# Attention backward loop: one hand-written order of PE's work for another

## The chip, the cores and the metric

The kernel runs on one core of a Trainium2 chip. The time is the device time of one launch, in microseconds (us); the kernel before took 2461.13 us, the median of three runs (2459.82 to 2464.63).

A core has five engines, each with its own queue of instructions that it takes in order. PE (TensorE) multiplies matrices and writes PSUM; ACT (ScalarE) computes functions such as the exponential; DVE (VectorE) works elementwise; POOL (GpSimd) does elementwise work on SBUF; SP (SyncE) issues DMAs. ACT issues DMAs too, from the same queue as its computing. The engines run side by side and wait for each other by semaphores. [...]

## The reference

The kernel computes a transformer block with adaptive layer norm and the gradients of all its inputs but one:

```
mod = (silu(c) @ w_mod).reshape(c.shape[0], 6, 1, -1)       # sa, ca, ga, sb, cb, gb
h = layernorm(x) * (1 + ca) + sa
x = x + ga * attention(h, wqkv, wo)                          # 32 heads of 16, no mask
h = layernorm(x) * (1 + cb) + sb
x = x + gb * (relu(h @ w1 + b1) ** 2 @ w2 + b2)
out, vjp = jax.vjp(f, A_x, A_wqkv, A_wo, B_w1, B_b1, B_w2, B_b2, c, w_mod)
return (out, *vjp(grad_out))
```

There are 2048 tokens of 512 features, and the MLP has 1792. Inputs and outputs are bf16. The part that matters here is the gradient of the attention. For each head, with scores S = q k^T / 4 and their softmax P, and with dP = dO v^T less a sum per row, it needs P again, dS = P * dP, and from them dV = P^T dO, dK = dS^T q and dQ = dS k.

## The kernel before

The first 1100 us are the forward pass and the MLP's gradients. Then the backward loop of the attention runs to about 2350 us, and the last 110 us finish the input and weight gradients. The change touches the backward loop alone.

**Tiling.** The 32 heads go in 8 groups (hg) of 4. A *unit* is one group, 128 queries (one of 4 qi in one of 4 qc) and 512 keys (kc). Four units with the same keys and neighbouring queries are a *block*; there are 512 units and 128 blocks. The four heads of a unit sit in four groups of 32 rows of the 128 partitions, so a head's matmul takes 32 rows.

**The steps of a unit, and the token that stands for each.**

- s0 to s15 (`score`): one matmul each, the scores of one head of one unit; s0 to s3 are the heads of the block's first unit, s4 to s7 of the second, and so on. A score goes to one of three PSUM banks, A, B or C, by a letter per token behind the order.
- e0 to e15 (`expo`): ACT reads such a bank, takes the exponential and writes E_u in SBUF as bf16. The row sums of the forward pass are already in the operands, so E is P.
- D (`dp_pair`): PE computes dP of two heads into a PSUM tile psD (there are two), and DVE multiplies it with E into dS_u. The Ds run behind: the first D of a block is the second pair of the last unit of the block before, the other seven belong to the block itself up to the first pair of its last unit. After the second pair of some units, SP issues a DMA that transposes dS into dsT (`transpose_unit`).
- q: alternately `k_quad` (k, four matmuls, dS times q) and `v_quad` (v, four matmuls, E times dO), each on four groups of 32 columns, both summed in the bank accVK. The qs run further behind, the first of a period being k of the third unit of the block before. After every 16 units ACT copies accVK to vkb.
- t1, t2 (`pe_turn`): in every second block one unit's dS is transposed on PE instead, in two halves of eight 128 x 128 transposes each, into bank C; T1 and T2 are ACT's copies of these into dsT.
- d1, d2 (`dq_quad`): two halves of eight matmuls, dS^T times k for the block two before, into bank C; Q (`dq_out`) is ACT's copy to dqtmp, which POOL adds to dQacc. At the end of a head group, POOL's result dQst is stored to DRAM by four DMAs that ACT issues.
- f (`keep_warm`): one matmul with zeros, which changes no result.

**The order.** All this is under a manual schedule: the loop at L1783 goes through the tokens of a block in the written order and each call puts its instructions on its engine's queue. Blocks alternate between `order_t`, which has t1, t2, T1, T2 and f, and `order_n`, which has none of them; the two are one period, and there are 64 periods. As each engine takes its own queue in order, a token binds only the tokens of the same engine ahead of it and behind it; everything else is data, or a bank or buffer that must be free. Bank C serves a score, a turn or dQ in turn, and in the stretches where it holds a turn or dQ the scores have A and B alone.

**Loads and stores on ACT's queue.** The operands of the next head group, the stores of vkb and those of dQst are put on ACT's queue through a list of due times (`at`, `todo`), which is counted in Ds: after the n-th D, what is due at n is issued. `dq_out` books the four stores of a finished head group at 6, 7, 8 and 9 Ds after its own place.

The lines of the loop that dispatch the tokens:

```
for b in range(NU // 4 + 3):
    toks, bank = order_t if on_pe(b - 1) else order_n
    for tok in toks:
        c, i = tok[0], int(tok[1:] or 0)
```

Of the kernel before, what the change touches and what calls it, by code (L numbers as in the profile page):

```python
# [21 lines left out]
D = 512  # L22
# [12 lines left out]
def kernel(  # L35
# [1546 lines left out]
    with ExitStack() as ph:  # L1582
# [9 lines left out]
        def load_head(hg):  # L1592
            st = dict(hsets[hg % 2])
            st["qz"] = qz[hg % 2]
            st["acc"] = stg.tile([P, n], F32, name="dQacc", tag="dQacc", bufs=1)
            st["dq"] = stg.tile([P, n], BF, name="dQst", tag="dQst", bufs=1)
            st["vk"] = stg.tile([P, n], BF, name="vkb", tag="vkb")
            hst[hg] = st
# [140 lines left out]
        def dq_out(b):  # L1739
# [21 lines left out]
                    at(cur["j"] + 6 + hq, load, dQc[hg // 2, r:r + DH, :], st["dq"][32 * hq:32 * hq + DH, :])  # L1761

        order_t = (
            "s0 s1 q s2 e0 e1 D s3 D e2 s4 e3 q t1 e4 T1 D "
            "s5 s6 e5 f f t2 e6 s7 T2 e7 D s8 e8 D f f s9 e9 q q s10 "
            "s11 e10 D d1 d2 e11 Q q s12 D e12 s13 e13 q s14 D e14 "
            "s15 q q e15 ").split(), "ABCABBABACABABCA"
        order_n = (
            "s0 D s1 q e0 q s2 e1 e2 D s3 s4 q s5 e3 D e4 "
            "e5 s6 q s7 D s8 e6 e7 d1 e8 s9 D d2 e9 q Q s10 "  # L1770
            "s11 e10 D q s12 e11 e12 s13 e13 D q s14 s15 e14 e15 D q ").split(), "CBACBACBABABCABC"
        load_head(0)
        for hg in range(1, HG):
            plan_head(hg)
# [332 lines left out]
```

## Time and profile before

One execution was profiled. It took 2461.76 us, with a span of 2460.0 us from its first to its last instruction.

| what | value |
|---|---|
| median of three runs | 2461.13 us |
| profiled execution; its span | 2461.76 us; 2460.0 us |
| busy over the span: PE, ACT, DVE, POOL | 94%, 93%, 75%, 20% |
| mean granted clock of PE | 0.990 |
| exponentials (E_u): number, mean of one in banks A, B, C | 2048; 651, 642, 647 ns |
| dS multiplies: number, mean of one | 1024; 1218 ns |
| copies of a turn (dsT): number, mean of one | 126; 1055 ns |
| copies of dQ (dqtmp): mean of one | 629 ns |
| copies of accVK (vkb): number, mean of one | 32; 688 ns |

An instruction's duration reaches from its start to its end, and on ACT the next one starts before the last has ended: exponentials of 0.65 us end 0.49 us apart. Durations must therefore not be added up; the distance between ends tells what one costs. PE's matmuls overlap in the same way, and their ends are modelled, so its busy share tells little of how much room it has. The name ahead of the arrow is what an instruction writes, the one behind what it reads; a releaser in square brackets is what ended the idle time ahead of it.

### The profile page before, as it was taken

The numbers are of one execution on the slowest core, as the hardware profiler recorded it, in microseconds if no ns is written. First come the engines' busy times: TensorE is split into PE (matmuls) and PEld (weight loads), VectorE is DVE, ScalarE is ACT, GpSimd is POOL, SyncE is SP. The second block draws the span as 40 slices with busy tenths as digits, with TensorE's granted clock in tenths as the row PEclk, the third lists the DMA queues.
The fourth block names the chain that finished last, engine by engine and source line by source line (L and its number), as shares of the span: only waits on it lengthen the run. The fifth ranks groups of instructions, "written<-read, shape, count | busy, mean of one in ns | idle before, by whom it ended". The sixth has DMA issues, their size and how long they took to land.

```text
span 2460.0 us, 49911 instructions
## 1 busy us (share of the span) xinstructions
PE 2308.8 (94%) x18994; PEld 776.1 (32%) x18994; DVE 1846.2 (75%) x2393; ACT 2298.6 (93%) x3559; POOL 489.5 (20%) x661
## 2 busy tenths in 40 slices
PE   8899999989998999899999999999999999999999
PEld 3232223233322333442322323332232332323254
DVE  6555463455445554669999999999899999999975
ACT  7999999999999999639999999999999999999964
POOL 2111222432544353200111101111011010110100
PEclk9999999999999999999999999999999999999999
DMA  4468554266647774989999999999999999999995
GB/s 149 130 171 189 182 140 103 85 161 142 97 91 154 152 139 89 239 244 189 206 198 207 199 212 199 208 196 207 198 201 208 207 206 201 209 195 219 200 261 180
DMA packets 1192303, 440.58 MB, mean 179 GB/s; under 512 B 1068283, under 2 KB 1161913, under 8 KB 1191550
## 3 DMA queue, kind: packets, MB, share of 16 engines
q1 hardware_dynamic: 1155214, 392.23, 81.0%
q0 software_dynamic: 19872, 27.09, 6.9%
q10 hardware_dynamic: 16976, 18.07, 3.0%
q8 instruction: 149, 2.44, 0.4%
q14 instruction: 92, 0.75, 0.1%
HBM read 98.83 MB, written 72.63 MB: 70 GB/s over the span
## 4 chain that ended last, share of the span: by engine, by line
ACT 39%; PE 36%; issue 10%; DVE 8%; DMA 6%; POOL 1%; ACTq 0%; SPq 0%; DVEq 0%; POOLq 0%
ACT E_u L1634 24%; ACT ET L580 12%; PE dqacc L1736 4%; PE psST L578 3%; PE psS_A L1628 3%; DMA dsT<-dS_u 3%; PE accVK L1709 2%; PE pm L234 2%; PE psS_B L1628 2%; PE oacc L594 2%; PE psS_C L1628 2%; PE pm L502 2%; PE pdh L1929 2%; PE pm L412 2%; PE pwq L1962 2%
## 5 line engine op out<-in xcount | busy, mean ns | idle before, releaser
L1650 DVE TENSOR_TENSOR dS_u<-psD_u,E_u 128x1024 bf16<-128x1024 f32 x1024 | 1185.6, 1218 | 63.4 <-PE psD_u L1648 17.4
L580 ACT ACTIVATE ET<-psST 128x1024 bf16<-128x1024 f32 x1024 | 942.4, 1248 | 12.4 <-PE psST L578 12.1
L1634 ACT ACTIVATE E_u<-psS_A 128x512 bf16<-128x512 f32 x768 | 499.8, 651 | 8.2 <-PE psS_C L1628 6.8
L1634 ACT ACTIVATE E_u<-psS_B 128x512 bf16<-128x512 f32 x768 | 493.1, 642 | 11.6 <-DMA dsT<-dS_u 4.6
L1648 PE MATMUL psD_u<-iv,ido 32*128 32x512 bf16 x2048 | 409.2, 386 | 0.3 <-DVE dS_u L1650 0.2
L578 PE MATMUL psST<-qt_sb,kt_sb 32*128 32x512 bf16 x2048 | 311.2, 386 | 39.4 <-ACT ET L580 35.0
L1634 ACT ACTIVATE E_u<-psS_C 128x512 bf16<-128x512 f32 x512 | 331.5, 647 | 3.4 <-PE psS_B L1628 1.1
L1628 PE MATMUL psS_B<-ik,iq 32*128 32x512 bf16 x768 | 293.0, 381 | 13.8 <-ACT E_u L1634 6.2
L1628 PE MATMUL psS_A<-ik,iq 32*128 32x512 bf16 x768 | 292.0, 380 | 13.2 <-DVE dwlast L238 0.9
L1757 POOL TENSOR_TENSOR dQacc<-dQacc,dqtmp 128x512 f32<-128x512 f32 x64 | 81.2, 1269 | 846.3 <-ACT dqtmp L1752 846.3
L1628 PEld LDWEIGHTS <-iq 32*128 32x128 bf16 x2048 | 130.8, 91 | 323.8 <-issue 308.2
L1709 PE MATMUL accVK<-dS_u,qz 128*32 128x512 bf16 x2048 | 213.4, 389 | 0.2 <-DVE dS_u L1650 0.2
L594 PE MATMUL oacc<-ET,vaug 128*32 128x512 bf16 x2048 | 207.1, 395 | 3.9 <-DVE ostage L598 3.9
L1718 PE MATMUL accVK<-E_u,dOs_tok 128*16 128x512 bf16 x2048 | 202.3, 384 | 0.0
L1628 PE MATMUL psS_C<-ik,iq 32*128 32x512 bf16 x512 | 194.2, 379 | 3.9
L578 PEld LDWEIGHTS <-kt_sb 32*128 32x128 bf16 x2048 | 84.2, 91 | 318.2 <-issue 298.6
L1736 PE MATMUL dqacc<-dsT,KS_tok 128*32 128x512 bf16 x2048 | 145.8, 382 | 15.5 <-ACT E_u L1634 1.5
L252 DVE COPY part<-pm 128x512 f32<-128x512 f32 (+2 forms) x106 | 65.2, 615 | 119.2 <-PE pm L234 114.1
L1648 PEld LDWEIGHTS <-ido 32*128 32x128 bf16 x2048 | 106.0, 91 | 96.9 <-issue 84.8
L1821 ACT ACTIVATE dsT<-ptT 128x1024 bf16<-128x1024 bf16 x126 | 132.9, 1055 | 0.1
L1709 PEld LDWEIGHTS <-qz 128*32 128x32 bf16 x2048 | 58.6, 94 | 176.3 <-issue 161.3
L594 PEld LDWEIGHTS <-vaug 128*32 128x32 bf16 x2048 | 53.2, 93 | 121.9 <-issue 121.9
(421 smaller groups left out, 2659.9 us busy)
## 6 DMA issues: line engine op xcount, KB each, us to landing
p_st<-part POOLq DMA_DIRECT2D x36, 256.0 KB, 4.6
kt_sb<-qkT_st POOLq DMA_DIRECT2D x124, 64.0 KB, 3.2
wA<-in_B_w_dram SPq DMA_DIRECT2D x28, 256.0 KB
wB<-w1T_st SPq DMA_DIRECT2D x21, 256.0 KB
wA<-w2T_st SPq DMA_DIRECT2D x21, 256.0 KB
wB<-in_B_w_dram SPq DMA_DIRECT2D x21, 256.0 KB
p_st<-part POOLq DMA_DIRECT2D x28, 192.0 KB, 5.1
p_st<-part SPq DMA_DIRECT2D x18, 256.0 KB
```

Source lines behind the costliest of these rows:

```text
L578: PE.matmul(ps[:, hi, :], kt_sb[r:r + 32, kt * P:(kt + 1) * P], qt_sb[r:r + 32, :], start=True, stop=True, tile_position=(r, 0))
L580: ACT.activation(ET[:, 2 * pair:2 * pair + 2, :], ps[:], AF.Exp, scale=SCALE)
L594: PE.matmul(oacc[32 * hq:32 * hq + 32, :], lhsT, ET[:, hq, :], start=(kt == 0), stop=(kt == TT - 1), tile_position=(0, 32 * hq), skip_grou ...
L1628: PE.matmul(psS[:], st["q"][r:r + 32, qt * P:(qt + 1) * P], st["k"][r:r + 32, kc * 512:kc * 512 + 512], start=True, stop=True, tile_positi ...
L1634: ACT.activation(bst[u][0][:, hq, :], sst.pop((u, hq))[:], AF.Exp, scale=SCALE)
L1648: PE.matmul(psD[:, hi, :], st["do"][r:r + 32, qt * P:(qt + 1) * P], st["v"][r:r + 32, kc * 512:kc * 512 + 512], start=True, stop=True, til ...
L1650: DVE.tensor_tensor(dS_u[:, 2 * pair:2 * pair + 2, :], psD[:], E_u[:, 2 * pair:2 * pair + 2, :], ALU.mult)
L1709: PE.matmul(cur["vk"][32 * hq:32 * hq + 32, :], hst[hg]["qz"][:, qt, hq, :], bst[u][1][:, hq, :], start=(qt == 0), stop=False, tile_positi ...
L1718: PE.matmul(acc[32 * hq:32 * hq + DH, :], dOs_tok[:, qt, (hg * 4 + hq) * DH:(hg * 4 + hq + 1) * DH], E_u[:, hq, :], start=False, stop=(qt ...
L1736: PE.matmul(acc[32 * hq:32 * hq + 32, :], KS_tok[:, kc * 4 + kt, h * DH:h * DH + 32], tT[:, :, hq * 4 + kt, :], start=(kt == 0), stop=(kt ...
L1757: POOL.tensor_tensor(dst2, dst, tmp[:], ALU.add)
L1821: ACT.activation(dst, pt[:], AF.Identity)
```

## The change

Both strings of tokens are written anew. The letters that give the banks, the functions and everything else are the same. The numbers of tokens are the same too but for f, of which `order_t` has five instead of four, and q, of which it has seven instead of eight while `order_n` has nine instead of eight; over a period there are sixteen qs as before.

```
         order_t = (
-            "s0 s1 q s2 e0 e1 D s3 D e2 s4 e3 q t1 e4 T1 D "
-            "s5 s6 e5 f f t2 e6 s7 T2 e7 D s8 e8 D f f s9 e9 q q s10 "
-            "s11 e10 D d1 d2 e11 Q q s12 D e12 s13 e13 q s14 D e14 "
-            "s15 q q e15 ").split(), "ABCABBABACABABCA"
+            "s0 s1 f e0 s2 e1 q s3 e2 s4 e3 D D t1 f q f e4 s5 D T1 s6 "
+            "e5 t2 q e6 T2 f D s7 s8 e7 e8 f D s9 e9 q D s10 s11 d1 "
+            "e10 d2 s12 e11 D Q s13 e12 q e13 s14 D e14 q s15 q e15 ").split(), "ABCABBABACABABCA"
         order_n = (
-            "s0 D s1 q e0 q s2 e1 e2 D s3 s4 q s5 e3 D e4 "
-            "e5 s6 q s7 D s8 e6 e7 d1 e8 s9 D d2 e9 q Q s10 "
-            "s11 e10 D q s12 e11 e12 s13 e13 D q s14 s15 e14 e15 D q ").split(), "CBACBACBABABCABC"
+            "s0 s1 D q e0 e1 q s2 s3 e2 D q e3 s4 s5 D e4 s6 e5 e6 q q "
+            "s7 D e7 s8 d1 s9 e8 e9 D d2 s10 D Q s11 e10 e11 q s12 e12 "
+            "q D s13 e13 s14 q e14 D s15 q e15 ").split(), "CBACBACBABABCABC"
```

In PE's sequence, the first D of a period now stands behind s4 instead of s2; t1 is followed by f, v, f and only then s5; where two qs stood together, mostly one stands now; v of the block's last unit before comes ahead of the sixth D; and k behind d2 has gone to behind s13 in `order_t` and behind s11 in `order_n`.

## The prediction

> **What bounds the kernel now.** The page's first part first, then busy time by stretches of the backward loop (1130 to 2350 us).
>
> ```profile
> PE 2308.8 (94%) x18994; PEld 776.1 (32%) x18994; DVE 1846.2 (75%) x2393; ACT 2298.6 (93%) x3559; POOL 489.5 (20%) x661
> ...
> 1200.00:1300.00 100.00, 96.44 (x926) 29.98 (x922) 95.54 (x84) 98.59 (x190) 11.43 (x9) 1.00 1.18 204
> 1900.00:2000.00 100.00, 96.49 (x940) 30.21 (x933) 95.66 (x84) 98.79 (x190) 11.62 (x8) 1.00 1.18 209
> ```
>
> In the loop three engines look full: PE 96, DVE 96, ACT 99 of 100 us, at clock 1.00. So the shares do not say which is the limit, and I went to the timeline. I call a block run by order_t T, one run by order_n N; two blocks are a period and there are 64. The turns' copies give the period: the first one starts at 1515.65 and again at 1534.83, 19.18 us. Over 59 periods the median is 19.18 without the copy vkb and 19.34 with it, the mean 19.44.
>
> ACT's ends: exponentials follow each other by 0.49 (the copies of dqacc and accVK too), a turn's copy by 0.917. So a period without vkb needs 32 x 0.49 + 2 x 0.917 + 2 x 0.49 = 18.49 on ACT. 0.69 is lost, nearly always in the same five places. Two of them in T, then two in N:
>
> ```profile
> 1519.38 0.69 ACT L1634 ACTIVATE E_u<-psS_C 128x512 bf16<-128x512 f32 x1
> ...
> 1520.04 0.60 ACT L1634 ACTIVATE E_u<-psS_A 128x512 bf16<-128x512 f32 x1
> 1520.12 1.05 PE L1736 MATMUL dqacc<-dsT,KS_tok 128*32 128x512 bf16 x16
> 1520.53 0.59 ACT L1634 ACTIVATE E_u<-psS_B 128x512 bf16<-128x512 f32 x1
> ...
> 1521.28 0.60 ACT L1752 ACTIVATE dqtmp<-dqacc 128x512 f32<-128x512 f32 x1 [0.15 <-PE dqacc L1736]
> ...
> 1508.21 0.61 PE L1736 MATMUL dqacc<-dsT,KS_tok 128*32 128x512 bf16 x8
> 1508.45 0.69 ACT L1634 ACTIVATE E_u<-psS_A 128x512 bf16<-128x512 f32 x1
> 1508.76 0.38 PE L1628 MATMUL psS_B<-ik,iq 32*128 32x512 bf16 x1
> 1509.18 0.60 ACT L1634 ACTIVATE E_u<-psS_B 128x512 bf16<-128x512 f32 x1
> 1509.80 0.60 ACT L1752 ACTIVATE dqtmp<-dqacc 128x512 f32<-128x512 f32 x1
> ```
>
> T: e9 leaves bank C at 1520.07, d1 starts in it 0.05 later, both halves run, and Q ends at 1521.88, 1.81 after e9, where e10, e11 and Q alone need 1.47. N: d1 holds PE when s9 is due; s9 starts at 1508.76, e9 ends 1.02 later, 0.15 late; Q then waits 0.11. Medians: e10 of T 0.08, Q of T 0.23 (only without vkb), e0 of N 0.08 (its bank C is left by e14, two before), e9 of N 0.15, Q of N 0.11: together 0.65. These are waits for a bank, not for PE's load.
>
> PE's load: priced by groups that did not wait, the T order takes 8.6 and the N order 6.6, 15.2 of 19.18. PE counts as busy because its matmuls overlap.
>
> SP is the fourth full engine:
>
> ```profile
> L1669 SPq DMA_TRANSPOSE dsT<-dS_u x191: 4821/5332/7152, 1111.3 to 2344.3; - x191
> L1667 SPq DMA_TRANSPOSE dsT<-dS_u x63: 1836/2846/4053, 1127.8 to 2336.8; - x63
> ```
>
> 3 x 5.33 + 2.85 + 4 gaps of 0.1 = 19.2 per period, so SP runs 0 to 10 us behind DVE. And once per head the four stores of dQst disturb ACT:
>
> ```profile
> 1282.85 1.10 ACTq L1610 DMA_DIRECT2D dQc<-dQst  x1
> ...
> 1284.00 0.60 ACT L1634 ACTIVATE E_u<-psS_B 128x512 bf16<-128x512 f32 x1 [0.53 <-issue]
> ...
> 1752.56 3.85 SPq L1667 DMA_TRANSPOSE dsT<-dS_u  x1
> ...
> 1756.56 0.31 ACTq L1610 DMA_DIRECT2D dQc<-dQst  x1
> ...
> 1756.92 0.60 ACT L1634 ACTIVATE E_u<-psS_B 128x512 bf16<-128x512 f32 x1 [4.05 <-DMA dsT<-dS_u]
> ```
>
> The fourth store waited for a transpose to land; that period took 24.70. Summed over all periods, what lies above 19.18 and 19.34 is 10.8 us. That is all that a better order could win.
>
> **The change part by part.** Each engine sees only its own tokens. ACT's e0 to e15, T1 (after e4), T2 (after e6) and Q (after e11 in T, e9 in N) stand in the same sequence before and after, so the exponentials are not reordered on ACT. DVE's 16 multiplies, SP's transposes and POOL's adds keep their sequence. What changes is PE's sequence, one more keep-warm matmul f in T (5 for 4), and between which ACT instructions the ACT-issued DMAs fall.
>
> Prices on PE, start to start: row-tiled group (s, D) to column-tiled one (q, f, d) 0.30; q to q 0.22; column to row 0.33; t to a row group 0.55; matmuls of different row groups start together, a second one on the same group 0.2 later. A bank or psD buffer is taken 0.05 after it is left; an exponential ends 1.02 after its score starts, if it waits; a dS multiply starts 0.54 after its D (1521.32, 1521.86) and the next follows by 1.13.
>
> *The five waits.* T: "s9 ... s10 s11 d1 d2" still puts both halves ahead of Q, and d1 is free to start when e9 leaves C: the D that now stands before s10 ends that group 0.13 before. N: "s8 d1 s9 D d2" is the same. s0 of N still waits for e14. So all five stay: 0.
>
> *q singly, f added.* Row segments per period go from 16 to 19 and PE's load to about 16.6 (three more streams of 0.21, six more changes of mode at 0.10, f 0.22). Covered by PE's 4 us of waiting, unless a score comes late. So I went through every score of the new order, from the release of its bank to its exponential's turn on ACT. Room is left by at least 0.1 everywhere but here:
> - e5 of T. s4 starts 0.05 after e1; the second D behind it shares its row group, 0.2; t1 0.31 later; t1 to f is in no row, between d's 0.44 and 0.55; f to v 0.22, v to f 0.22, f to s5 0.33, then 1.02: 2.79 to 2.90. ACT arrives after e2, e3, e4, T1, e5: 1.47 + 0.917 + 0.49 = 2.88. Late by 0 to 0.02. Before, no f stood there and s5 came straight behind t1 and D.
> - e7 of N. s6 0.05 after e3, k 0.30, v 0.22, s7 0.33, 1.02: 1.92 of 1.96. In time by 0.04.
> - d1 of N, behind an s8 that shares D's row group: 0.09 before e6 leaves C.
> - s10 of T, behind a D that needs a psD buffer. T's first D now stands behind s4 and its multiply starts 0.6 later than before (DVE idles there 0.9 instead of 0.35); the multiplies follow from there by 1.13, so the D ahead of s10 (the sixth) waits to about 0.05 after s10's bank is free. e10 comes 0.05 late, and Q, late by 0.23 anyway, takes that up; with vkb between e9 and e10 it is hidden.
>
> I take 0.02 per period for the first, as t to f changes between 128-wide and 16-wide tiles and is nearest to the 0.55: 64 x 0.02 = 1.3 us. With every step at its largest (0.1 more on each of the first three) they give 0.12 + 0.06 + 0.01 = 0.19, 12 us; the lower end is 0, since the five waits bar a gain here.
>
> *DVE and SP.* DVE needs 16 x 1.13 = 18.1 of 19.18, so the later start is made up within T, where DVE idled before (medians 0.18, 0.16 and 0.46, ahead of the third, fourth and sixth multiply behind t1). T's pair of units 0 and 1 reaches SP 0.5 later, and where SP had caught up it starts 0.5 later. The landing is next wanted by d1 two blocks on, some 8 us after it. Cost 0.
>
> *Stores and loads on ACT's queue.* In N, Q now stands behind one more D, and the stores are counted in Ds: each falls one D later. The first stood behind T1 with a load just ahead of it, and e5 was late by 0.63 in four heads and 0.40 in one: 2.9 us. It now stands alone behind T2, whose 0.917 covers it: -2.9. The fourth now meets a load, between e11 and Q of T: the two take 0.34 + 1.10 there at worst, against 0.49 + 0.23 of room, +0.7 x 6 = +4.2, at best 0. I take 0 for both together, ends -2.9 and +4.2. The fourth store's long wait (5.5 us once) depends on how far SP is behind: 0, ends -5.5 and +5.5.
>
> Sum: 2461.76 (profiled execution: span 2460.0 and 1.76 around it) + 1.3 = 2463.1. The median of the three runs, 2461.13, is 0.6 below it: **2462.5 us**.
>
> **Rivals.**
> 1. *Slower: s5 comes late.* One mechanism: t1, f, v, f stand between s4 and s5, where t1 and D stood. If t to f or the shared row group costs 0.1 to 0.2 more than priced, e5 is late in all 64 periods; it decides from 0.08 on (5 us). At 0.15: 9.6 us, 2471. For it: that path has no slack by my own prices, and t to f was never seen. Against: the largest rows give 2.90 of 2.88.
> 2. *Slower: PE becomes the bound.* 40 mode changes for 34, each 0.10, three more streams, one f: 1.4 per period, 90 us, 2551. For it: PE at 96%. Against: PE's groups fill 16.6 of 19.18. [...]
> 3. *Slower by SP.* Where SP starts 0.5 later in every period and does not catch up, more stores wait as at 1756: two more are 11 us, 2472.
> 4. *Faster.* The disturbances at the heads go: first stores 2.9 and the long wait 5.5, 2453. For it: both hang on where the stores fall. Against: only 10.8 us are there, and half came once.
>
> **How the numbers follow.** Forecast (within 0.2%, 5 us, about what a measurement of this kernel tells from no change; own range 2457 to 2466): 0.42. Rival 1: 0.28; rival 2: 0.04; rival 3: 0.06; rival 4: 0.20. So faster 0.20, same 0.42, slower 0.38. The low end is rival 4, 2453; the high end the largest steps and stores, 12 + 4 above: 2477. Outside: rival 2 and parts of 1 and 4.
>
> **What would show it.** Periods of 19.18 and 19.34 again and the five waits unchanged; e5 of T at most 0.05 late; DVE idle by 0.9 behind s4; PE with 64 more matmuls; no e5 wait of 0.63 at the heads. Wrong, if a sixth wait stands in every period, above all at e5 of T or e7 of N, or if the periods fall below 19.18.

## The result and the profile after

The changed kernel takes 2477.38 us (median of six runs, 2474.27 to 2486.59), the kernel before beside it 2459.56 (2458.33 to 2464.63). The ratio is 1.0074, with a 95% interval of 1.0060 to 1.0088: 0.74% slower, 17.8 us, where no measurable change was forecast and 2477 was the high end of the range. The measured time lies just above it.

The profiled execution took 2486.59 us, the longest of the six, so its single losses are above the average. First two lines of the page (busy time; the granted clock of PE in 40 slices), then busy time by stretches of the loop: PE, PEld (weight loads), DVE, ACT and POOL, each with its number of instructions, then the granted clock, the share of the DMA engines and GB/s.

```profile
PE 2325.6 (94%) x18972; PEld 772.5 (31%) x19058; DVE 1836.4 (74%) x2393; ACT 2300.9 (93%) x3559; POOL 489.3 (20%) x661
...
PEclk9999999999999999989999999989999899999999
```

```profile
1200.00:1300.00 100.00, 95.16 (x917) 29.20 (x913) 93.18 (x82) 96.97 (x186) 11.40 (x9) 0.98 1.17 203
1900.00:2000.00 100.00, 94.78 (x849) 27.60 (x847) 86.31 (x76) 90.97 (x172) 9.11 (x6) 0.90 1.15 191
```

The 64 further matmuls f show in the number of weight loads (PEld): 19058, before 18994. The number of PE's matmuls, 18972, is below that of its loads, so some matmuls are missing from the record.

In the same two stretches both clocks were 1.00 before; now they are 0.98 and 0.90, and ACT has fallen from 99 to 91 us of 100 in the second. The loop has four stretches at half clock, 61.4 us together. The kernel before had one, of 6.83 us at 1756.82, behind the wait of the fourth store:

```profile
1753.41:1756.82 3.41, 0.60 (x11) 0.10 (x4) 0.22 (x1) 0.00 (x0) 0.00 (x0) 1.00 1.15 152
1756.82:1760.24 3.42, 2.68 (x21) 0.45 (x20) 2.10 (x2) 3.05 (x6) 0.00 (x0) 0.50 1.15 222
1760.24:1763.65 3.41, 3.41 (x25) 0.50 (x21) 2.73 (x3) 2.54 (x6) 0.00 (x0) 0.50 1.08 200
1763.65:1767.06 3.41, 3.32 (x43) 0.94 (x39) 3.15 (x3) 3.37 (x8) 0.00 (x0) 1.00 1.22 214
```

**The steady periods are as they were.** Without the copy vkb the median period is 19.19 us, with it 19.35 (before: 19.18 and 19.34). The timeline of a block N (the first three lines) and of a block T (the last four), ACT alone; the columns are start, duration, engine, line, operation:

```profile
1518.43 0.64 ACT L1634 ACTIVATE E_u<-psS_A 128x512 bf16<-128x512 f32 x1
1519.11 0.60 ACT L1634 ACTIVATE E_u<-psS_B 128x512 bf16<-128x512 f32 x1
1519.74 0.60 ACT L1752 ACTIVATE dqtmp<-dqacc 128x512 f32<-128x512 f32 x1
...
1529.37 0.64 ACT L1634 ACTIVATE E_u<-psS_C 128x512 bf16<-128x512 f32 x1
1530.00 0.60 ACT L1634 ACTIVATE E_u<-psS_A 128x512 bf16<-128x512 f32 x1
1530.50 0.59 ACT L1634 ACTIVATE E_u<-psS_B 128x512 bf16<-128x512 f32 x1
1531.21 0.60 ACT L1752 ACTIVATE dqtmp<-dqacc 128x512 f32<-128x512 f32 x1
```

In T, Q ends at 1531.81, 1.80 after e9 (before: 1.81); in N, e9 is 0.15 late and Q 0.14 again. The medians of the five waits are 0.10, 0.23, 0.08, 0.15 and 0.14, and there is no sixth.

**The loss stands at the head boundaries.** What lies above 19.18 and 19.34, summed over all periods, has grown from 10.8 us to 31.7. The timeline of the first boundary:

```profile
1288.47 3.85 SPq L1667 DMA_TRANSPOSE dsT<-dS_u  x1
...
1292.00 0.40 PE L1709 MATMUL accVK<-dS_u,qz 128*32 128x512 bf16 x4
...
1292.85 0.36 ACTq L1610 DMA_DIRECT2D iqs<-q_st  x1
1293.25 0.58 ACTq L1610 DMA_DIRECT2D dQc<-dQst  x1
1293.87 0.60 ACT L1749 ACTIVATE dQacc<-dqacc 128x512 f32<-128x512 f32 x1 [2.23 <-issue]
...
1294.52 0.37 PE L1628 MATMUL psS_C<-ik,iq 32*128 32x512 bf16 x1 [2.13 <-ACT dQacc L1749]
...
1295.48 2.36 DVE L1650 TENSOR_TENSOR dS_u<-psD_u,E_u 128x1024 bf16<-128x1024 f32 x2 [2.04 <-ACT E_u L1634]
```

Behind e11, ACT's queue now holds a load and the fourth store, and Q behind both. The trace gives each DMA's semaphore. The 1196 DMAs that SP and ACT issue in it, taken together, go round eight of them (101, 102, 103, 105, 106, 107, 109, 110) in the same turn from first to last, and before the change they did so too. The load at 1292.85 has 110, as has the transpose that SP issued from 1283.34 to 1288.42, eight DMAs earlier. That transpose landed at 1292.83, so the load starts at 1292.85, Q at 1293.87 instead of 1291.6, and s14, which needs bank C, holds all of PE for 2.13 us. At the six boundaries with both DMAs Q came late by 2.33, 0.90, 2.56, 0.99, 3.10 and 1.04: 10.9 us. Before, the DMA that met this transpose was the fourth store, ahead of e11: it has 110 there, the transpose landed at 1287.89 and the store starts at 1287.91.

Then the clock falls. The same columns in windows of 3.41 us:

```profile
1289.85:1293.27 3.42, 2.23 (x32) 0.91 (x29) 3.42 (x4) 1.79 (x4) 0.00 (x0) 1.00 1.20 156
1293.27:1296.68 3.41, 2.06 (x24) 0.69 (x23) 1.37 (x3) 2.81 (x6) 0.00 (x0) 1.00 1.27 272
1296.68:1300.09 3.41, 3.41 (x29) 0.64 (x21) 3.41 (x4) 3.21 (x7) 0.00 (x0) 0.50 1.21 201
...
1306.92:1310.33 3.41, 3.41 (x19) 0.61 (x17) 2.10 (x2) 2.54 (x6) 0.00 (x0) 0.50 1.67 204
1310.33:1313.75 3.42, 3.42 (x24) 1.13 (x20) 2.02 (x2) 2.52 (x4) 0.00 (x0) 0.50 0.86 93
1313.75:1317.16 3.41, 3.29 (x30) 1.14 (x30) 2.75 (x4) 2.88 (x6) 0.00 (x0) 1.00 0.46 112
```

For 17.07 us PE runs at 0.50 and reads 100% busy, and ACT gets 2.5 to 3.2 us of work in the windows shown. The two other long waits (1610.61, 1931.18) were followed by 20.48 us each. Over the six runs the mean granted clock is 0.983, in 35 runs of the kernel before it is 0.991: 2 x 0.0084 x 2477 = 42 us more at half clock (a microsecond at half clock lowers the sum by half a microsecond). Within the runs of this kernel and of e1, e3, e5 and e11 below, which have both new orders, the time rises by 0.35 to 0.44 us for each us at half clock; 42 of these are 15 to 18 us, nearly the whole loss. This price is a correlation and includes the stalls, as a stall and the stretch behind it come together.

### The profile page after: what moved, and what is told of

It reads as the page before. It is cut to its first block, busy times and chain, and to the rows that moved or that the text cites. A ratio compares the mean times of both kernels' runs of the same rounds, so it can differ in the third digit from the quotient of the medians.

```text
span 2484.4 us, 49950 instructions
## 1 busy us (share of the span) xinstructions
PE 2325.6 (94%) x18972; PEld 772.5 (31%) x19058; DVE 1836.4 (74%) x2393; ACT 2300.9 (93%) x3559; POOL 489.3 (20%) x661
## 4 chain that ended last, share of the span: by engine, by line
PE 51%; ACT 25%; DVE 12%; issue 6%; DMA 5%; ACTq 0%; POOL 0%; SPq 0%; DVEq 0%; another core or an unknown queue 0%; POOLq 0%
ACT ET L580 13%; ACT E_u L1634 10%; DVE dS_u L1650 5%; PE psS_B L1628 4%; PE accVK L1709 4%; PE dqacc L1736 4%; PE psS_A L1628 4%; PE psST L578 3%; PE accVK L1718 3%; PE psD_u L1648 3%; PE psS_C L1628 3%; PE accVK L1675 2%; DMA dsT<-dS_u 2%; PE ptT L1682 2%; PE pm L234 2%
## 5 line engine op out<-in xcount | busy, mean ns | idle before, releaser
L1634 ACT ACTIVATE E_u<-psS_A 128x512 bf16<-128x512 f32 x768 | 486.1, 633 | 16.0 <-PE psS_C L1628 6.9
L1634 ACT ACTIVATE E_u<-psS_B 128x512 bf16<-128x512 f32 x768 | 483.9, 630 | 11.7 <-PE psD_u L1648 9.0
L1648 PE MATMUL psD_u<-iv,ido 32*128 32x512 bf16 x2048 | 393.8, 392 | 14.0 <-DVE dS_u L1650 14.0
L1628 PE MATMUL psS_A<-ik,iq 32*128 32x512 bf16 x768 | 298.1, 388 | 1.9 <-ACT E_u L1634 1.1
L1718 PE MATMUL accVK<-E_u,dOs_tok 128*16 128x512 bf16 x2048 | 219.5, 391 | 0.0
L1628 PE MATMUL psS_C<-ik,iq 32*128 32x512 bf16 x512 | 199.2, 389 | 18.8 <-ACT dQacc L1749 9.7
L1648 PEld LDWEIGHTS <-ido 32*128 32x128 bf16 x2048 | 97.1, 91 | 141.3 <-issue 127.0
L1675 PE MATMUL accVK<-dOs_tok,KS_tok 128*16 128x512 bf16 x330 | 128.3, 389 | 0.0
L1709 PEld LDWEIGHTS <-qz 128*32 128x32 bf16 x2048 | 53.0, 93 | 170.5 <-issue 163.8
```

The lines of the kernel that those rows point to most:

```text
L1628: PE.matmul(psS[:], st["q"][r:r + 32, qt * P:(qt + 1) * P], st["k"][r:r + 32, kc * 512:kc * 512 + 512], start=True, stop=True, tile_positi ...
L1634: ACT.activation(bst[u][0][:, hq, :], sst.pop((u, hq))[:], AF.Exp, scale=SCALE)
L1648: PE.matmul(psD[:, hi, :], st["do"][r:r + 32, qt * P:(qt + 1) * P], st["v"][r:r + 32, kc * 512:kc * 512 + 512], start=True, stop=True, til ...
L1675: PE.matmul(cur["vk"][0:DH, :], KS_tok[:, 0, D:QPAD], dOs_tok[:, 0, :], start=False, stop=False, tile_position=(0, 0), skip_group_check=True)
L1709: PE.matmul(cur["vk"][32 * hq:32 * hq + 32, :], hst[hg]["qz"][:, qt, hq, :], bst[u][1][:, hq, :], start=(qt == 0), stop=False, tile_positi ...
L1718: PE.matmul(acc[32 * hq:32 * hq + DH, :], dOs_tok[:, qt, (hg * 4 + hq) * DH:(hg * 4 + hq + 1) * DH], E_u[:, hq, :], start=False, stop=(qt ...
```

## The experiments

From here, e1 to e18 are the kernels of the experiments; where the exponential of that name is meant, the text says "token e5". A is the theory that the places of the loads and stores on ACT's queue make the loss, B that PE's new order itself does. The kernel before ran beside each set of experiments (2459.5 to 2460.7); differences are against that, and "clock" is the mean granted clock over a kernel's runs.

### Where the stores stand

```
e1 (new orders)   at(cur["j"] + 5 + hq, load, dQc...)        # 6 + hq
e2 (old orders)   at(cur["j"] + 7 + hq, load, dQc...)
e3 (new orders)   at(cur["j"] + 7 + 4 * hq, load, dQc...)
e4 (old orders)   at(cur["j"] + 8 + 4 * hq, load, dQc...)
```

> The new order, with the four stores of dQst booked one D earlier (5 to 8 Ds behind Q instead of 6 to 9), so that they fall at the same counts of Ds from the start of a block as before the change. The tokens, and so PE's, DVE's, SP's and POOL's sequences, are those of the new order; only ACT's queue differs, at the eight head boundaries. Theory A (the loss is a load and a store on ACT's queue just ahead of Q, which wait for a transpose's landing; PE idles over 2 us behind Q and then runs at half clock): the load still stands ahead of Q, but the DMA that is eight behind the late transpose is now the fourth store, between e9 and e10. It waits there instead; two scores are then still ready for ACT but PE waits for their banks. I expect most of the loss back, 2460 to 2468, and at most one head with PE at half clock. Theory B (the new sequence on PE itself, with three more streams of 128-wide groups and one more f, leaves too little room after any disturbance): 2474 to 2480, as with the change.

> The old order, with the four stores booked one D later (7 to 10 Ds behind Q), which is what the change did to them in its first block. PE's sequence is that of the kernel before. Theory A: the four stores then stand behind T2, e8, e10 and Q of T; the fourth, which stands right behind a load, is behind Q and not ahead of it. The load behind Q, before e12, meets the late landing (waits of 2 to 3 us less one instruction, 0.5). PE holds the scores of e12 and e13 ready, so ACT alone stands; 2460 to 2468. Theory B: 2457 to 2461, as before, since PE's order is the old one.

> The new order, with the four stores four Ds apart (7, 11, 15, 19 Ds behind Q), halfway between the loads, so that no two DMAs meet on ACT's queue and the DMA eight behind the late transpose comes a block later. Theory A: nothing ahead of Q of T but the load, which then meets a transpose that is landed: the heads' periods near 19.3 to 20, no granted clock below 1 at the heads, 31.7 us of excess over 19.18 and 19.34 falls to 5 to 12: 2450 to 2460. Theory B: 2470 to 2480.

> The old order with the same spread of the stores (8, 12, 16, 20 Ds behind Q: the same places from the start of a block as in the new order with 7, 11, 15, 19). Theory A: the old order's own excess at the heads, 10.8 us, falls to 2 to 6: 2451 to 2457, and the two orders then differ by less than 5 us. Theory B: 2457 to 2461, and the new order with spread stores is 10 us or more slower.

| kernel | median us (range) | ratio to before (95%) | clock |
|---|---|---|---|
| e1 | 2469.42 (2460.85 to 2485.18) | 1.0044 (1.0024 to 1.0064) | 0.987 |
| e2 | 2461.36 (2456.48 to 2467.39) | 0.9998 (0.9985 to 1.0012) | 0.991 |
| e3 | 2466.91 (2455.30 to 2480.66) | 1.0031 (1.0012 to 1.0049) | 0.986 |
| e4 | 2463.69 (2459.85 to 2467.35) | 1.0008 (0.9995 to 1.0020) | 0.989 |

Moving the stores gives back about half of the loss and no more. e1 and e3 lie between the ranges that A and B expected; they scatter over 25 us, and their times follow the clock. e2 lies in the range of A and 0.4 us above that of B, and tells little. So neither theory holds alone.

e3 and e4 missed in a second way: their profiles have no wait above 0.4 us at the first six head boundaries, and yet e4 is not faster than the kernel before. Its timeline shows what comes in their place, away from any boundary:

```profile
1966.61 2.63 SPq L1667 DMA_TRANSPOSE dsT<-dS_u  x1
1969.33 11.14 SPq L1669 DMA_TRANSPOSE dsT<-dS_u  x2
...
1974.30 0.94 PE L1736 MATMUL dqacc<-dsT,KS_tok 128*32 128x512 bf16 x8 [2.04 <-DMA iv<-vT_st]
...
1975.81 0.60 ACT L1634 ACTIVATE E_u<-psS_B 128x512 bf16<-128x512 f32 x1 [2.50 <-PE psD_u L1648]
```

d1 of a block N waits 2.04 us. The profile names a load that landed at about that time; what d1 reads is the transpose issued at 1966.61, which landed at 1974.16. SP was 4 to 9 us behind DVE there, with 0.09 us between transposes; at the same time in the kernel before it was 0.7 to 5 us behind. Over the loop from 1300 to 2300 its mean lag is 3.7 us, before 2.8. e3 is alike: its one wait of PE over 0.6 us in the loop is d1's (2.14 us at 2252), and the mean lag is 4.8. The reading that fits is that the waits at the boundaries were SP's time to catch up: without them SP falls behind until PE waits for it. By it the 10.8 us were not to be won by moving the stores.

### PE's order and ACT's queue apart

In e5 and e6 the DMAs due are no longer issued behind a D but behind a fixed number of ACT's tokens, so that ACT's queue is that of the other kernel: e5 has the new orders on PE and all of ACT's queue from before, with the same semaphores, e6 the old orders and the new queue. (e6 also books the stores of vkb 3 Ds behind their copy instead of 4, which keeps them where the changed kernel has them.) In both traces the 204 loads and stores on ACT's queue come in the sequence, and with the semaphores, of the kernel whose queue they take.

```
+            due_t, due_n = [2, 2, 6, 10, 11, 13, 15, 17], [0, 3, 4, 6, 9, 12, 15, 17]   # e5
+            due_t, due_n = [4, 4, 5, 9, 11, 12, 14, 17], [0, 3, 4, 7, 10, 10, 14, 16]   # e6
...
                         nD += 1
-                        cur["j"] = nD
-                        for j in sorted(j for j in todo if j <= nD):
-                            for f, args in todo.pop(j):
-                                f(*args)
...
+                    if c in "eTQ":
+                        nA[0] += 1
+                        act_dmas(places)
```

> PE's sequence of the changed kernel with ACT's whole queue of the kernel before: loads and stores are issued after the same ACT instructions as before the change and wait for the same semaphores. What is left of the change is PE's order alone. Theory A (the places of loads and stores on ACT's queue make the loss): as the kernel before, within 4 us of its median. Theory B (PE's new order keeps the clock at half for longer after any disturbance; stretches at half clock so far: 3.4 and 6.8 us with the old order, 6.8 to 23.9 with the new one): 4 to 12 us above it, mean granted clock near 0.987.

> PE's sequence of the kernel before with ACT's whole queue of the changed kernel: a load and the fourth store stand ahead of Q at the head boundaries. Theory A: the loss of the changed kernel, 12 to 18 us above the kernel before, with Q late by 2 to 3 us at half of the heads. Theory B: Q is as late, but PE is back at full clock after 3.4 to 6.8 us: 3 to 8 us above the kernel before.

| | ACT's queue before | ACT's queue new |
|---|---|---|
| PE's orders before | 2459.87, clock 0.991 | e6: 2470.55, 1.0041 (1.0025 to 1.0057), 0.986 |
| PE's orders new | e5: 2468.33, 1.0037 (1.0017 to 1.0058), 0.986 | 2477.38, 1.0074 (1.0060 to 1.0088), 0.983 |

The two parts cost 10.7 and 8.5 us alone and 17.8 together (against its own runs of before). e5 lies in the range that B expected, e6 between A's 12 to 18 and B's 3 to 8: both theories are half right. In e6 the load and the store hold Q with the old orders too:

```profile
1447.51 0.35 ACTq L1610 DMA_DIRECT2D iqs<-q_st  x1
1447.89 0.75 ACTq L1610 DMA_DIRECT2D dQc<-dQst  x1
1448.69 0.60 ACT L1749 ACTIVATE dQacc<-dqacc 128x512 f32<-128x512 f32 x1 [2.68 <-issue]
...
1449.33 0.37 PE L1628 MATMUL psS_C<-ik,iq 32*128 32x512 bf16 x1 [2.42 <-ACT dQacc L1749]
```

In e5 the fourth store stands between token e10 and token e11 as before the change, and waits there:

```profile
1291.92 0.34 ACTq L1610 DMA_DIRECT2D dQc<-dQst  x1
1292.31 0.60 ACT L1634 ACTIVATE E_u<-psS_B 128x512 bf16<-128x512 f32 x1 [1.45 <-DMA dsT<-dS_u]
...
1292.96 0.55 PE L1628 MATMUL psS_B<-ik,iq 32*128 32x512 bf16 x1 [1.24 <-ACT E_u L1634]
```

PE idles 1.24 us only, and 23.89 us at half clock follow. Before, the wait of 4.05 us in the same place of a later boundary, in which PE idled 3.55 us, was followed by 6.83 us.

### The same stall in both orders

Q of T copies its bank seven times at chosen blocks, 6 x 0.49 = 2.94 us more. e7 and e8 do it once per head, at the same distance from each boundary.

```
-                ACT.activation(tmp[:], acc[:], AF.Identity, scale=SCALE)
+                for _ in range(7 if b % 16 == 8 else 1):                     # e7, e8
+                for _ in range(7 if b % 6 == 0 and b % 16 >= 4 else 1):      # e14 to e18
+                    ACT.activation(tmp[:], acc[:], AF.Identity, scale=SCALE)
```

> The kernel before; once per head, in the middle of it (8 times in all), Q of T copies its bank seven times instead of once: ACT is held for 6 x 0.49 = 2.94 us, bank C with it, and PE runs out of work as at the heads of the changed kernel. Nothing else changes. PE idles 1.5 to 2.5 us and the clock may fall. Theory B: 8 x (2.9 + 0 to 1.5), 23 to 36 us above the kernel before, less what the pauses of SP's backlog give back; stretches at half clock of 3.4 to 6.8 us.

> The changed kernel with the same forced stall, 8 times. Theory B: each stall costs 2.9 and 4 to 7 more, 8 x 7 to 10 = 56 to 80 us above the changed kernel, with stretches at half clock of 17 to 24 us in most of the eight places. Theory A (the order has no part in how long half clock lasts): the same surplus as the old order shows, 23 to 36 us.

e7 took 2503.96 us (2502.54 to 2507.57), 44 above the kernel before or 5.5 for each stall, where 23 to 36 were expected. e8 took 2521.64 (2507.11 to 2543.38), also 44 above the changed kernel: between A's 23 to 36 and B's 56 to 80. The pair says little, though. How long the clock stayed down went with where in a window of 3.41 us the stall began (the windows' bounds follow from the clock's changes in the same trace: in the profile before the change all 19 changes, and in the one after it all 27, lie on one grid of 3.413 us to within 0.001 us). In the profile of e8 six of the eight stalls begin in the first third of a window, and two windows at half clock follow each; one begins 0.90 through a window, and six follow. As 160.4 us are 47.0 windows, a run can meet the same phase again and again, which may be why the runs of e8 lie 36 us apart. And in that profile the boundaries are calmer (Q 0.5 to 1.4 late), so the base is another one. e14 and e15 therefore take sixteen stalls in changing phase, and e15 has ACT's queue of before.

> The kernel before with sixteen forced stalls, every third period where the head allows it: Q of T copies its bank seven times, 2.94 us more. They fall in changing phase against the windows of the clock, so that one profile shows the spread of the stretches at half clock that one and the same stall brings. From the eight stalls before: 5.5 us for each, 88 us above the kernel before; stretches of 3.4 to 13.7 us, mean 7 to 8.

> The new orders on PE, ACT's queue as before the change, with the same sixteen stalls. If a stall of the same size keeps the clock at half for longer with the new orders (theory B): stretches of 6.8 to 23.9 us, mean 12 to 14, and 16 x 7.7 = 120 us and more above the kernel before. If only the number of stalls that reach half clock differs: the same stretches and 88 us above the new orders without stalls.

e14: 2558.64 us (2553.02 to 2560.32), 98 above the kernel before, 6.1 for each stall (88 and 5.5 were expected). e15: 2599.13 (2593.28 to 2604.58), 131 above e5, 8.2 for each. So the new orders make the same stall dearer by a third, as B expected. The first stall below is from e14, the second from e15, each at a place where the stretches begin alike:

```profile
1885.92:1889.33 3.41, 0.45 (x8) 0.19 (x5) 1.22 (x1) 3.25 (x6) 0.00 (x0) 1.00 1.18 240
1889.33:1892.74 3.41, 2.71 (x20) 0.46 (x23) 1.23 (x1) 2.67 (x7) 1.26 (x1) 0.50 1.06 208
1892.74:1896.16 3.42, 3.42 (x25) 0.47 (x17) 2.81 (x3) 2.99 (x6) 0.00 (x0) 0.50 0.31 69
1896.16:1899.57 3.41, 3.41 (x27) 0.66 (x27) 2.42 (x3) 2.14 (x5) 0.00 (x0) 0.50 1.23 229
1899.57:1902.98 3.41, 3.41 (x32) 0.64 (x24) 2.65 (x3) 2.67 (x6) 1.27 (x1) 0.50 0.60 113
1902.98:1906.40 3.42, 3.28 (x32) 0.98 (x29) 2.92 (x3) 3.35 (x8) 0.00 (x0) 1.00 1.17 219
```

```profile
1583.99:1587.40 3.41, 0.37 (x5) 0.16 (x5) 1.02 (x1) 3.22 (x7) 0.00 (x0) 1.00 1.17 218
1587.40:1590.81 3.41, 2.88 (x20) 0.64 (x23) 1.22 (x1) 2.63 (x6) 1.26 (x1) 0.50 0.61 127
1590.81:1594.23 3.42, 3.42 (x25) 0.56 (x21) 3.07 (x3) 3.00 (x6) 0.00 (x0) 0.50 0.50 52
1594.23:1597.64 3.41, 3.41 (x27) 0.51 (x23) 1.93 (x3) 1.95 (x5) 0.00 (x0) 0.50 1.10 206
1597.64:1601.05 3.41, 3.41 (x25) 0.54 (x17) 2.35 (x2) 2.54 (x5) 1.26 (x1) 0.50 0.68 129
1601.05:1604.47 3.42, 3.42 (x19) 0.60 (x15) 2.45 (x2) 2.46 (x5) 0.00 (x0) 0.50 1.26 219
1604.47:1607.88 3.41, 3.41 (x24) 1.25 (x24) 1.55 (x2) 2.61 (x5) 0.00 (x0) 0.50 0.95 179
1607.88:1611.29 3.41, 3.41 (x31) 1.05 (x29) 2.98 (x3) 3.02 (x6) 0.00 (x0) 1.00 0.00 0
```

The first three windows at half clock hold 20, 25 and 27 matmuls in both (those running at the edges are counted twice). The fourth lies behind the ds of N: 32 with the old orders, and the clock is back; 25 with the new ones, and it stays down through the start of T until t1 (the window of 1604.47). The mean stretch that begins before 2400 is 9.8 us in e14 and 15.0 in e15.

The new orders do not lengthen every stretch. Fifteen of the sixteen stalls lie in the loop. Behind those that begin in the first third of a window, 2 to 4 windows at half clock follow with the old orders and 2 with the new ones; behind those in the last third, 1 to 6 (mean 3.8) with the old and 6 to 7 (mean 6.5) with the new.

### Which string

> PE's new order_t with the old order_n (order_t gets the sixteenth q at its end, as the old one has it), ACT's queue as before the change. What is to be told apart is where the longer stretches at half clock come from. In the traces so far a window of 3.41 us in which PE starts fewer than about 25 matmuls is followed by a window at half clock, and at half clock the windows behind a stall in T hold 20, 21, 23, 24, 28 with the old order and 20, 21, 23, 21, 15, 23, 30 with the new one, which misses the end in N. Theory B1 (the second half of the new order_n, where s11 and s12 stand alone between qs, has too few matmuls per window at half clock): as the kernel before, 0 to 4 us above it. Theory B2 (order_t makes it): 6 to 10 us above it, as with both new.

> PE's old order_t with the new order_n (without its first q, which the old order_t holds at its end), ACT's queue as before the change. Theory B1: 5 to 10 us above the kernel before, with stretches at half clock of 17 us and more. Theory B2: 0 to 4 us above.

> Both new orders with ACT's queue as before the change, and in each block one token moved back: the k that stood behind s13 (order_t) and s11 (order_n) stands right behind d2 again, in the same tiling as d2. That leaves one change of tiling less in each block, and s11 and s12 of order_n stand together. Theory B1: at half clock the window behind the ds of N holds 24 or more again, stretches end after 3 to 14 us, and the time is 0 to 4 us above the kernel before. Otherwise 6 to 10 us above it.

> Of the change, order_n and the first half of order_t (up to the D ahead of s9) are new; from s9 on order_t is as before (with one q less at s9 and at the end, so that the sum stays sixteen). ACT's queue as before the change. Theory B3 (the second half of order_t: behind a waiting e11 or Q, PE finds fewer groups ahead of the next score that needs ACT, since the sixth D stands ahead of s10 and no q behind d2, so its windows fall below 25 matmuls more often): as the kernel before, 0 to 4 us above. Theory B4 (the first half: t1, f, q, f, q singly, where a stretch at half clock that comes from the block before has to end): 6 to 10 us above.

> Of the change, order_n and the second half of order_t (from s9 on) are new; its first half is as before. ACT's queue as before the change. Theory B3: 6 to 10 us above the kernel before. Theory B4: 0 to 4 us above.

All have ACT's queue of before. In short form, the tokens that differ from e5:

```
e9   order_t: new, "... e14 q s15 q q e15"      order_n: old
e10  order_t: old                               order_n: new, "s0 s1 D e0 e1 q ..."
e11  order_t: "... e10 d2 q s12 e11 D Q s13 e12 e13 ..."
     order_n: "... d2 q s10 D Q s11 e10 e11 s12 e12 q D ..."
e12  order_t: new up to s9, then "s9 e9 q s10 s11 e10 D d1 d2 e11 Q q s12 D e12 s13 e13 q s14 D e14 s15 q e15"
e13  order_t: old up to s9, then "s9 e9 q q D s10 s11 d1 e10 d2 s12 e11 D Q s13 ..." as new
```

| kernel | median us (range) | ratio to before (95%) | clock |
|---|---|---|---|
| e9 | 2478.32 (2467.06 to 2481.73) | 1.0066 (1.0043 to 1.0090) | 0.987 |
| e10 | 2459.22 (2456.30 to 2468.81) | 0.9997 (0.9984 to 1.0010) | 0.991 |
| e11 | 2469.61 (2462.11 to 2488.82) | 1.0037 (1.0018 to 1.0057) | 0.987 |
| e12 | 2464.02 (2455.50 to 2468.39) | 1.0008 (0.9993 to 1.0022) | 0.990 |
| e13 | 2461.32 (2456.20 to 2470.35) | 1.0008 (0.9994 to 1.0022) | 0.990 |

e10 is the kernel before again, so order_n alone costs nothing here, and B1 falls. e9 is slow. Part of that is its own: the q put at the end of order_t makes the steady periods 19.24 and 19.54 instead of 19.18 and 19.34, 29 x 0.06 + 30 x 0.20 = 7.7 us; some 10 remain, as in e5. e11 shows that the moved k is not it. Either half of order_t with the new order_n costs 0.08%, with intervals that hold zero and end at 0.22%; both halves together cost 0.37% (0.17 to 0.58). So neither B3 nor B4 is confirmed, as each expected 6 to 10 us from one half. Whether the halves add up or cost something only together, these intervals do not tell.

Then the sixteen stalls in the mixed orders:

> Order_n and the first half of order_t new, ACT's queue as before, with the sixteen stalls. What is to be told apart is which part makes a stretch at half clock longer for the same stall (mean 9.8 us with the old orders, 14.5 with the new ones; 98 and 131 us more than without stalls). If order_n does (its windows behind the ds hold 21 matmuls at half clock where the old ones hold 24): stretches as with both new, 2590 to 2600. If the second half of order_t does: 2555 to 2570. If it takes the first half of order_t, where the long stretches end: 2585 and more.

> Order_n and the second half of order_t new, with the sixteen stalls. If order_n makes the stretches longer: 2590 to 2600. If the second half of order_t does: 2585 and more; if the first: 2555 to 2570.

> Order_n alone new, with the sixteen stalls. If order_n makes the stretches longer: 2590 to 2600, with windows of 21 behind the ds of N and of 15 to 20 at the start of T. If order_t does, in either half: 2555 to 2570, as with the old orders.

| orders under sixteen stalls | median us (range) | above before | mean stretch in the profile, us |
|---|---|---|---|
| e14: both old | 2558.64 (2553.02 to 2560.32) | 98 | 9.8 |
| e18: order_n new | 2592.38 (2583.70 to 2599.68) | 133 | 18.5 |
| e16: order_n and the first half of order_t new | 2601.19 (2594.56 to 2606.36) | 142 | 19.5 |
| e17: order_n and the second half of order_t new | 2576.59 (2570.86 to 2591.68) | 117 | 13.4 |
| e15: both new | 2599.13 (2593.28 to 2604.58) | 139 | 15.0 |

Order_n alone makes a stretch about twice as long: e18 came out where this was expected of order_n. e16 lies 1 us above that range and fits the first half of order_t as well (2585 and more); e17 lies between the ranges. The single means depend on phase: in e16 ten of fifteen stalls begin in the last third of a window, in e14 five. With each third of a window counted alike, the stretches behind the stalls are 10.0, 18.6, 16.3, 13.9 and 13.8 us, in the order of the table.

Without forced stalls order_n costs nothing (e10). The reading that fits is that too few stalls reach half clock there, and that order_t brings more of them. This is not shown: the mean clock of e9 is 0.987 and that of e10 0.991, but the profiled run of e9, its second fastest, has two stretches of 3.41 us in the loop, and that of e10 one of 17.07 and one of 3.41. Nor was the new order_t run with the old order_n under forced stalls. What stays open: which tokens of order_t cost the time, and which of order_n keep a window short of matmuls. In the second half of the new order_n, s11 and s12 stand alone between qs, where every score stood beside another or a D; e11 put these two together and did not help. No version here beats the kernel before.

## Why the prediction was wrong

- *The five waits, the periods, tokens e5 and e7*: right. 19.19 and 19.35; token e5 is late by 0.01 (median) where 0.02 was taken; DVE idles 0.91 behind s4 where 0.9 was said. Rival 1, the likeliest against the forecast, and rival 2 did not happen.
- *"each falls one D later", the first store*: right, the wait of token e5 at the boundaries is gone.
- *"the two take 0.34 + 1.10 there at worst, against 0.49 + 0.23 of room, +0.7 x 6 = +4.2, at best 0"*: this is the term that failed. It priced the load and the fourth store by their issue times, as if they were free to start. At each boundary one DMA there waits for a transpose to land, and the move put it from in front of e11 to in front of Q. Q came late by 0.90 to 3.10, 10.9 us, and e6 shows 10.7 us for the new places by themselves.
- *"The fourth store's long wait (5.5 us once) depends on how far SP is behind: 0"*, and rival 3: the wait was seen, but put down to SP's lag. SP was no later: this transpose lands 26.0 us behind t1 of the block before on average, and 25.8 before the change. What changed is what is queued behind the wait: token e11, with PE still holding work, or Q and bank C, without which PE stops.
- *The granted clock*: no step of the sum held it. The two stretches of 100 us that the prediction shows were at 1.00; the one with the store at 1756 was not:

```profile
1700.00:1800.00 100.00, 93.51 (x891) 28.48 (x887) 91.02 (x79) 94.00 (x180) 8.39 (x7) 0.97 1.18 200
```

Its 0.97 is the 6.83 us at half clock. The prediction priced a stall at its own length. With the old orders a stall of 2.94 us costs 5.5 to 6.1, with the new ones 8.2. PE's order, taken as free, cost 8.5 us in e5, whose mean clock was 0.986 against 0.991 before.
- *"q singly, f added ... Covered by PE's 4 us of waiting"*: right at full clock, as the periods show, and blind to half clock, where PE reads busy for 3.41 of 3.41 us, as in the window at 1296.68.
- *"That is all that a better order could win"* (10.8 us): too much. In e4 the waits at the boundaries are gone and SP's backlog takes their place.
- *"the high end the largest steps and stores, 12 + 4 above: 2477"*: that this is nearly the measured time is luck. The 12 were scores late in every period, which lost about 0.01 each; the 4 were issue times. What was lost were waits for landings and time at half clock, and neither is in the 16.

## What to carry to other kernels

Here a DMA on a compute engine's queue was not an issue of 0.3 us but a wait of up to 4 us. So find the DMA whose semaphore it takes over, see when that one lands, and ask what stands behind the waiting DMA and who runs dry. A reorder that left the steady periods within 0.01 us still lost 17.8 us, at the few places that stall: after each of three long waits PE stayed at half clock for 17 to 20 us. So compare two orders by giving both the same stall, at changing phases, as in e14 and e15 (6.1 and 8.2 us for each). And where SP had 0.09 us between its transposes, taking the stalls at the boundaries away won nothing (e4 took 2463.69 us, the kernel before 2460.42): ask whether a stall pays for a backlog elsewhere before removing it.

## What the hardware showed

- Every stretch at half clock in the loop, in 20 traces, is a multiple of 3.41 us, 3.41 to 27.31. Half clock followed waits of PE that were shorter than one window of 3.41 us: 1.24 us (e5 at 1292.96), 2.13 (the changed kernel at 1294.52) and 2.42 (e6 at 1449.33).
- Windows that the profile shows as 100% busy stayed at 0.50, five in a row in e15 (from 1590.81) and six in e18 (from 1530.65); so the profile's busy share does not tell when full clock comes back. Counting the matmuls that start in a window of the loop, over all 20 traces: at full clock, 6332 windows with 25 or more were followed by half clock twice, 317 with fewer 111 times; at half clock, 37 windows with 25 or more ended the stretch 26 times, 384 with fewer 86 times. In these counts the clock goes with the number of matmuls. A window at full clock with fewer than 25, as in the expectation of e9, was thus followed by half clock in a third of the cases. Whether the clock follows this count or something that goes with it was not tried.
- In the traces before and after the change the 1196 DMAs of SP and ACT go round eight semaphores in one turn, so a load whose issue took 0.36 us on ACT's queue waited for a transpose that SP had issued eight DMAs earlier, and Q behind it came 2.33 us late (the changed kernel at 1292.85).
